# Allotting the twice-used buffers first, masking six more pairs by a bias matmul, and moving one piece of second products

## The chip, the cores and the metric

The kernel runs on one NeuronCore of a Trainium2 chip. The metric is the device time of one execution in microseconds (us), lower being better. The core has a matrix engine (TensorE, PE in the profile; its weight loads are listed apart as PEld), VectorE (DVE), ScalarE (ACT), GpSimd (POOL), SyncE (SP, which here only issues transfers) and 16 DMA engines. TensorE's results go to PSUM, eight banks of 128 x 512 float32; SBUF is the working memory of 128 partitions.

## The reference

Two blocks are computed one after the other. The first is attention with two branches over q, k and v of shape (8, 8, 576, 64): a coarse one on means of four positions, and a local one in which a position sees only those less than 4 away.

```python
q_d = q.reshape(B, H, Sd, factor, D).mean(axis=3)      # the same for k_d, v_d; factor = 4
out_up = np.repeat(sm_attn(q_d, k_d, v_d), factor, axis=2)
mask = np.abs(pos[:, None] - pos[None, :]) < factor
scores = np.where(mask, scale * np.matmul(q, k.transpose(0, 1, 3, 2)), -1000000000.0)
out = out_up + np.matmul(softmax(scores), v)
```

The second takes these outputs as x of shape (4608, 512) through two weight matrices of 512 x 2048 and 2048 x 512:

```python
h = x @ w_in
out = (h * (1.0 / (1.0 + np.exp(-h)))) @ w_out
```

## The kernel before

**Pairs.** The 64 heads are handled as 32 pairs p = 0 to 31, the two heads of a pair on the two halves of the partitions. For a pair, q and k (qkb, bf16) are transposed on TensorE (T), copied out by ScalarE (qT, kT, L583) and summed by fours on VectorE (qd, kd, L872); the scores of both branches are made by 64x64 matmuls (S, `pe_S`, L889); ScalarE takes their exponentials into Pt (local) and Pd (coarse) (L920); then come the row sums (Z), their transposes and reciprocals on VectorE (zt, r, b; L1015 to L1034), the products with v (PV), a multiply on VectorE (m, xo, L1050) and the sum of both branches on GpSimd (a, L1078), which writes the pair's part of xT. From pair 8 on these steps are bundled into visits V8 to V33 (`visit`, L1419): V(n) holds the scores of pair n, the products with v of pair n - 2, the row sums of pair n - 1 and the transposes of pair n + 1. So V31 holds the last scores, V32 the last row sums and V33 the last products with v.

**The local mask.** Scores outside the band have to vanish. For pairs below MB = 8 (L35) four matmuls come first in `pe_S`: nidn (a diagonal of -81920) against mbias (1 outside the band) puts a large negative number there, onto which the scores are added. For pairs from 8 on, Pt is multiplied by a mask of ones and zeros on VectorE after the exponential (k, L926).

**The dense part.** The 4608 rows are nine supertiles j = 0 to 8 of 512. A first product g1_j_f (L1089) is four float32 (fp32r) matmuls of 128x512, with a block of w_in as weights; its value is turned into gT by ScalarE (L1103) and VectorE (L1107). A second product g2_j_tt (L1343) is 16 bf16 matmuls in four pieces, with gT as weights and w_out as the moving operand; ScalarE copies it out (L1368) and SyncE stores it. First and second products fill TensorE between the visits.

**The last stage.** The first products of supertiles 7 and 8 are made from seven half-size products each for groups g = 0 to 7 (`prod`, P1_g to P7_g, two f32 matmuls each), with sums of blocks of w_in (S1 to S4, GpSimd, `sums`, L1169) and of xT (X1 on GpSimd, X2 to X4 on VectorE, L1166) as operands. `group` (L1233) has the copies and additions between them (p1, p5, c11, u4, c22, c12; L1236, L1237). P4_0 waits for X4 and for c22_0, which follows P7_0. `tail` (L1267) gives a fixed order of these products, in which LATE6 (L42) puts six pieces of second products of supertile 6 to fill gaps: (tt, part) = (2, 2) in group 0's step, (2, 3) and (3, 0) after it, and (3, 1), (3, 2), (3, 3) after group 1's products. `g2_part` (L1308) makes such a piece.

**Order.** A planner on the host (`Plan`) gives each step its engine, cost, due time, buffers and PSUM banks, and lists the steps of each engine; `pick` (L1523) chooses on TensorE. The program then runs each engine's list in order, with semaphores where data or buffers ask for it. So a change of one step's cost or needs can move others.

**Buffers.** SBUF is allotted in the order of the calls of `sb` (L525). Five buffers (w_in_sb, qk, vs, vq, qkb) are given back after being named, and w_in_f, qk_r, vs_r, vq_r and qkb_r get the same places under another type, for the sums of the last stage. They are the last to be allotted (L568 to L580), 142,304 bytes per partition behind w_out_bf, which is the first; w_out_bf is at a multiple of 64, and 142,304 is 32 more than one.

Of the kernel before, what the change touches and what calls it, by code (L numbers as in the profile page):

```python
# [31 lines left out]
VE, VDUE = 'ACT', 12  # L32
CAST2 = 4
SW = tuple(range(1, NPAIR))
MB = 8  # L35
LAG = 2
THR0 = 10
LEAD = 6
# [464 lines left out]
def bass_hourglass_attn__then__act_silu_kernel(  # L503
# [9 lines left out]
    with kctx:  # L513
# [11 lines left out]
        def sb(name, shape, dt, n=None):  # L525
            if n is None:
                return E(nc.sbuf_tensor(name, shape, dt))
            return [E(nc.sbuf_tensor(f"{name}{i}", shape, dt)) for i in range(n)]

        w_out_bf = sb("w_out_bf", [128, 16, 512], BF16)  # L530
        xT = sb("xT", [128, 4, XR], F32)
        gT = sb("gT", [128, 16, 512], BF16, 2)
# [31 lines left out]
        vsel = sb("vsel", [128, 3, 207], BF16)  # L564
        vend = sb("vend", [128, 2, 128], BF16)
        cv = sb("cv", [128, 16], F32)

        with contextlib.ExitStack() as early:  # L568
            E = early.enter_context
            w_in_sb = sb("w_in_sb", [128, 4, DFF], F32R)  # L570
            qk = sb("qk", [128, 2, 576], F32, N_QK)
            vs = sb("vs", [128, 10, 64], F32, N_VS)
            vq = sb("vq", [128, 4, 256], F32, N_VQ)
            qkb = sb("qkb", [128, 2, 576], BF16, N_QKB)
        E = kctx.enter_context
        w_in_f = sb("w_in_f", [128, 4, DFF], F32)
        qk_r = sb("qk_r", [128, 1152], F32R)
        vs_r = sb("vs_r", [128, 640], F32R, N_VS)
        vq_r = sb("vq_r", [128, 1024], F32R, N_VQ)
        qkb_r = sb("qkb_r", [128, 576], F32R, N_QKB)  # L580

        def copy(eng, e, out_, in_):
            return e.activation(out_, in_, AF.Copy) if eng == "ACT" else e.tensor_copy(out_, in_)  # L583
# [305 lines left out]
        def pe_S(p):  # L889
            s, bb = S("T", p), bank(("s", p))  # L890
            rl = [R(f"kT{s}"), R(f"qT{s}"), R(f"kTa{s}"), R(f"kTb{s}")]
            rd = [R(f"kd{s}"), R(f"qd{s}"), R(f"kdp{s}")]
            bias = p < MB
            if bias:
                for h in range(2):
                    for y in range(2):
                        mm(PS[half(y), bb[h], 0:288], nidn[half(h), :], mbias[half(h), y, :],
                           [R("nidn")] + [R(f"mb{i}") for i in range(4)], [rB[bb[h]]], True, False)
            for i in range(5):
                for h in range(2):  # L900
# [13 lines left out]

        def after_S(p):
            def exps(local):
                def emit(jb):
                    m, b = S("P", p), bank(("s", p))
                    d, a, e_, sc = (Pt[m], 0, 288, 0.125) if local else (Pd[m], 288, 504, 0.0078125)
                    P.op("ACT", lambda e: e.activation(d[:, :, :], PS[:, b[0]:b[1] + 1, a:e_], AF.Exp, scale=sc),  # L920
                         [rB[b[0]], rB[b[1]]], [R(f"P{m}" if local else f"Pd{m}")])
                return emit

            def emitk(jb):
                m = S("P", p)
                P.op(jb.ran, lambda e: e.tensor_tensor(  # L926
                    Pt[m][:, :, :], Pt[m][:, :, :], mask[:, :].unsqueeze(1).to_broadcast([128, 2, 288]), ALU.mult),
                    [R(f"P{m}")] + [R(f"mask{i}") for i in range(3)], [R(f"P{m}")])
            kw = dict(bank=[(("s", p), ())], take=[("P", p)], pre=[f"S{p}"], due=D(p, 6.0))
            J(f"x{p}", "ACT", 0.66, exps(True), **kw)  # L930
            J(f"xd{p}", "ACT", 0.54, exps(False), **kw)
            if p >= MB:
                J(f"k{p}", K_ENG, {"DVE": 0.46, "POOL": 1.2}, emitk, pre=[f"x{p}", "mask0", "mask1", "mask2"], use=[("P", p)], port=True,
                  due=D(p, 5.3))

# [331 lines left out]
        def tail():  # L1267
# [4 lines left out]
            for g in range(9):  # L1272
# [13 lines left out]
                    g2_lo(6)  # L1286
                if g == 1:
                    prod(g, 6, a(g), False)
                if g:
                    prod(g - 1, 4, a(g - 1), False)  # L1290
                if g < 8:
                    if not g:
                        prod(g, 2, z(g, 1), True)
                        for tt, part in LATE6[0]:
                            g2_part(LO - 1, tt, part)
                    if g != 1:
                        prod(g, 6, a(g), False)
# [10 lines left out]
        def g2_part(j, tt, part):  # L1308
            key = ("g", j, tt)

            def emit(jb):
                b = bank(key)[0]
                for f in parts(j, part):
                    mm(PS[:, b, :], gT[j % 2][:, f, 128 * tt:128 * tt + 128], w_out_bf[:, f, :],
                       [R(f"w_out{f // 4}"), R(f"g{j % 2}_{f}")], [rB[b]], f == 0, f == 15)
            chain(f"g2_{j}_{tt}_{part}", 0.866, emit, 4, [f"s{j}_{f}" for f in parts(j, part)], [(key, G2_BANKS(j))])

        def parts(j, part):
            return range(4 * part, 4 * part + 4) if j < LO else (2 * part, 2 * part + 8, 2 * part + 1, 2 * part + 9)
# [59 lines left out]
                        , bank=[(("q", p), T_BANKS(p)), (("k", p), T_BANKS(p))])  # L1379

        def sk(p):
            return dict(use=[("T", p)], pre=[f"{a}{b}{p}" for a in "em" for b in "qk"] + ["pads"] + (["nidn", "mb0", "mb1", "mb2", "mb3"] if p < MB else []), bank=[(("s", p), S_BANKS(p))])

        def zk(p):
            return dict(use=[("P", p)], pre=[f"k{p}" if p >= MB else f"x{p}", f"xd{p}"] + SELZ)

        def vk(p):
            return dict(use=[("P", p), ("vb", p), ("vd", p)], pre=[f"k{p}" if p >= MB else f"x{p}", f"xd{p}", f"cv{p}", f"vd{p}"])

        def merge(*ds):  # L1390
            o = {}
# [5 lines left out]
        def split(p):  # L1397
            J(f"T{p}", "PE", 0.42, lambda jb: pe_T(p), mm=36, kind="A", due=D(p, 8.5), **tk(p))
            after_T(p)
            if p >= SPLIT:  # L1400
                return
            J(f"S{p}", "PE", 0.46, lambda jb: pe_S(p), mm=28 + 4 * (p < MB), kind="A", due=D(p, 6.5), **sk(p))
# [16 lines left out]
        def visit(n):  # L1419
# [5 lines left out]
            if new:  # L1425
                nm = 28 * s + 36 * t + 32 * (pv is not None) + 24
            else:
                nm = 28 * s + 36 * t + 28 * (pv is not None) + 14 * (z is not None)
            if s:
# [166 lines left out]
```

## Time and profile before

| | us |
|---|---|
| median of 3 runs | 338.47 (336.92, 338.47, 339.60) |
| the profiled execution | 339.03 |
| its span in the profile | 337.1 |
| TensorE busy | 318.6 of it |
| f32 matmuls against w_in_sb, 504, busy | 128.4 |
| bf16 matmuls of second products, busy (page's group of 562) | 125.0 |
| masks on VectorE (L926), 24 | 20.8 |
| granted TensorE clock, mean | 0.985 |

The page gives for each engine the time in which an instruction of it was running. Times in the trace's timeline count from the start of the span. Matmul records overlap, since a matmul is started before the one ahead of it has drained, so the pace is read from one start to the next; a few records are missing. "Issue" is time in which an engine waited for nothing that the profile shows.

### The profile page before, as it was taken

To read this page: it belongs to the slowest core of one execution; us is meant where nothing else is said; L and a number is where in the kernel's file an instruction comes from. 1 tells how busy PE (TensorE), PEld (TensorE's weight loads), DVE (VectorE), ACT (ScalarE), POOL (GpSimd) and SP (SyncE) were. 2 spreads that over 40 slices of the span, in tenths; PEclk is the share of its full clock that TensorE was granted. 3 is DMA by queue.
4 is the path that set the end of the run, shared out by engine and by line. 5 is a ranking of instruction groups with operands and counts; after the bars stand their busy time and mean duration, and the time that the engine had idled before them with its cause. 6 is when DMAs were issued, how large, how long until landed. Compare 5 with 4: busy or idle time off the path is not lost.

```text
span 337.1 us, 11443 instructions
## 1 busy us (share of the span) xinstructions
PE 318.6 (95%) x4923; PEld 208.3 (62%) x4957; DVE 239.9 (71%) x405; ACT 189.9 (56%) x340; POOL 180.4 (54%) x237
## 2 busy tenths in 40 slices
PE   6766999999999999999999999999999999999996
PEld 2454677865555775577547755775567555676544
DVE  7758889755686976789679966997599877555400
ACT  4833856664644665476456646564566516765531
POOL 8466378417588668861687058804798482000000
PEclk9977999999999999999999999999999999999999
DMA  8999999997889967896398429600210010000042
GB/s 176 200 248 211 316 170 198 213 180 173 164 178 206 244 151 164 214 207 156 72 227 185 100 51 206 169 1 24 75 36 2 0 64 31 31 1 2 0 156 95
DMA packets 70669, 44.64 MB, mean 132 GB/s; under 512 B 45914, under 2 KB 63770, under 8 KB 70618
## 3 DMA queue, kind: packets, MB, share of 16 engines
q1 hardware_dynamic: 56714, 28.08, 32.0%
q0 software_dynamic: 13088, 15.36, 27.1%
q8 instruction: 39, 0.64, 0.8%
q10 hardware_dynamic: 816, 0.46, 0.6%
q14 instruction: 12, 0.10, 0.1%
HBM read 45.61 MB, written 9.44 MB: 163 GB/s over the span
## 4 chain that ended last, share of the span: by engine, by line
PE 89%; issue 4%; DVE 2%; ACT 2%; DMA 1%; POOL 1%; ACTq 0%; POOLq 0%
PE PS L589 85%; PE PS L837 3%; DVE xT L1166 2%; DMA qkb<-in_q_dram 1%; POOL xT L1078 1%; ACT qT L583 1%; ACT kT L583 0%; ACTq L738 0%; DVE xo L1237 0%; POOL gT L623 0%; DVE xo L1050 0%; DVE qkb L1237 0%; ACT Pt L920 0%; ACT Pd L920 0%; ACT osb L1336 0%
## 5 line engine op out<-in xcount | busy, mean ns | idle before, releaser
L589 PE MATMUL PS<-xT,w_in_sb 128*128 128x512 f32 x504 | 128.4, 403 | 0.5 <-DVE xo L1237 0.5
L589 PE MATMUL PS<-w_out_bf,gT 128*128 128x512 bf16 (+1 forms) x562 | 125.0, 373 | 3.7 <-issue 3.0
L589 PEld LDWEIGHTS PS<-xT,w_in_sb 128*128 128x128 f32 x504 | 92.3, 188 | 24.6 <-ACT osb L1368 1.0
L589 PEld LDWEIGHTS PS<-w_out_bf,gT 128*128 128x128 bf16 x592 | 54.7, 98 | 63.8 <-issue 5.2
L1103 ACT ACTIVATE th<-PS 128x512 f32<-128x512 f32 x112 | 67.0, 599 | 37.6 <-PE PS L589 23.5
L1107 DVE SCALAR_TENSOR_TENSOR gT<-th,PS 128x512 bf16<-128x512 f32 x112 | 74.1, 679 | 13.2 <-ACT th L1103 11.3
L1078 POOL TENSOR_TENSOR xT<-xo 128x576 fp32r<-128x576 f32 (+5 forms) x48 | 42.5, 900 | 27.6 <-DVE xo L1050 27.1
L583 POOL CAST vb<-vs 128x640 bf16<-128x640 f32 x32 | 23.0, 720 | 41.4 <-PE PS L589 39.2
L1368 ACT ACTIVATE osb<-PS 128x512 f32<-128x512 f32 x35 | 20.7, 597 | 42.3 <-PE PS L589 41.1
L1050 DVE TENSOR_TENSOR xo<-PS,Rb 128x720 f32<-128x720 f32 x32 | 28.8, 900 | 14.5 <-PE PS L589 14.3
L920 ACT ACTIVATE Pt<-PS 128x576 bf16<-128x576 f32 x32 | 20.9, 652 | 30.3 <-PE PS L589 30.3
L812 POOL TENSOR_TENSOR vt<-vq 128x512 f32<-128x512 f32 x24 | 31.4, 1308 | 6.8 <-DMA vq<-in_v_dram 6.6
L926 DVE TENSOR_TENSOR Pt<-Pt,mask 128x576 bf16<-128x576 bf16 x24 | 20.8, 865 | 17.9 <-ACT Pt L920 17.9
L1034 DVE STREAM_TRANSPOSE Rb<-zr 128x768 f32<-128x768 f32 x32 | 30.9, 964 | 0.2
L702 POOL DMA_DIRECT2D qkb<-in_k_dram x31 | 16.9, 547 | 17.1 <-PE PS L837 11.4
L583 ACT ACTIVATE qT<-PS 128x576 bf16<-128x576 bf16 x32 | 21.1, 660 | 8.3 <-PE PS L837 5.5
L872 DVE TENSOR_REDUCE qd<-qT 128x144 bf16<-128x576 bf16 x32 | 22.7, 711 | 2.8 <-ACT qT L583 2.8
L837 PE MATMUL PS<-idn,qkb 64*64 64x64 bf16 x1152 | 18.3, 198 | 6.2 <-issue 4.0
L872 DVE TENSOR_REDUCE kd<-kT 128x144 bf16<-128x576 bf16 x32 | 22.9, 716 | 0.0
L583 ACT ACTIVATE kT<-PS 128x576 bf16<-128x576 bf16 x32 | 21.1, 660 | 0.0
L1252 ACT ACTIVATE gT<-xo 128x512 bf16<-128x512 f32 x24 | 14.9, 627 | 10.5 <-DVE xo L1237 10.5
L702 POOL DMA_DIRECT2D qkb<-in_q_dram x31 | 17.7, 572 | 5.1 <-DMA vs<-in_v_dram 5.1
(86 smaller groups left out, 339.2 us busy)
## 6 DMA issues: line engine op xcount, KB each, us to landing
vs<-in_v_dram SPq DMA_DIRECT2D x124, 80.0 KB, 4.9
out_dram<-osb SPq DMA_DIRECT2D x35, 256.0 KB, 3.1
vq<-in_v_dram SPq DMA_DIRECT2D x24, 256.0 KB, 5.0
qkb<-in_q_dram POOLq DMA_DIRECT2D x31, 144.0 KB, 4.6
qkb<-in_k_dram POOLq DMA_DIRECT2D x30, 144.0 KB, 5.1
w_in_sb<-in_moe_w_in_dram POOLq DMA_DIRECT2D x4, 1024.0 KB, 8.4
w_out_bf<-in_moe_w_out_dram POOLq DMA_DIRECT2D x4, 512.0 KB, 12.9
vq<-in_v_dram SPq DMA_DIRECT2D x48, 32.0 KB, 4.8
```

The lines of the kernel that those rows point to most:

```text
L583: return e.activation(out_, in_, AF.Copy) if eng == "ACT" else e.tensor_copy(out_, in_)
L589: P.op("PE", lambda t: t.matmul(out_, lhsT, rhs, start=start, stop=stop, skip_group_check=True), r, w, after=fence[:])
L702: P.op(j.ran, lambda s: s.dma_start(out_(), in_()), r() if r else [], w(), sem(), after=gates(hold))
L812: P.op("POOL", lambda g: g.tensor_tensor(vt[:, :, :], vq[n][:, :, 0:128], vq[n][:, :, 128:256], ALU.add), [R(f"vqm{n}"), R(f"vqe{n}0"), R( ...
L837: P.op("PE", lambda e, o=o, w=w, j=j: e.transpose(o, w, idn[half(j), :]), [R("idn"), R(f"qkb{n}{x}")], [rB[t]])
L872: P.op("DVE", lambda e: e.tensor_reduce(dst, src.rearrange("p (g r) -> p g r", r=4), AX.X, ALU.add), [R(f"{'qk'[x]}T{s}")], [R(f"{'qk'[x]} ...
L920: P.op("ACT", lambda e: e.activation(d[:, :, :], PS[:, b[0]:b[1] + 1, a:e_], AF.Exp, scale=sc), [rB[b[0]], rB[b[1]]], [R(f"P{m}" if local ...
L1034: P.op("DVE", lambda e: e.transpose(Rb[n][:, :].rearrange("p (c q) -> p c q", q=32), zr[z][:, :].unsqueeze(2).to_broadcast([128, 24, 32])) ...
L1050: P.op("DVE", lambda e: e.tensor_tensor(xo[x][:, :, :], PS[:, bb[0]:bb[1] + 1, 0:360], Rb[u][:, :].rearrange("p (x c) -> p x c", x=2)[:, : ...
L1078: P.op("POOL", lambda g, dst=dst, in0=in0, in1=in1: g.tensor_tensor(dst, in0, in1, ALU.add), [R(f"xo{x}")], xblk(kc, t + a, t + e_))
L1103: P.op("ACT", lambda e: e.activation(th[x][:, :], PS[:, b, :], AF.Tanh, scale=0.5), [rB[b]], [R(f"th{x}")])
L1107: P.op("DVE", lambda e: e.scalar_tensor_tensor(gT[j % 2][:, f, :], th[x][:, :], 1.0, PS[:, b, :], ALU.add, ALU.mult), [rB[b], R(f"th{x}")] ...
```

## The change

Three things are changed. The five twice-used buffers and their second names are allotted ahead of everything else instead of behind it; they move to multiples of 64, and all that was ahead of them moves up by 69,632 bytes, a multiple of 64. MB becomes a set: pairs 14, 18, 22, 26, 30 and 31 are masked by the bias matmuls too, and their multiplies on VectorE go. One of the three pieces behind group 1, (3, 1), is placed ahead of P4_0, and a piece of `g2_part` now names the piece before it as needed. The costs that the planner is given follow (0.13 more for a visit with a bias).

```diff
-MB = 8
+MB = tuple(range(8)) + (14, 18, 22, 26, 30, 31)
...
+        with contextlib.ExitStack() as early:
+            E = early.enter_context
+            w_in_sb = sb("w_in_sb", [128, 4, DFF], F32R)
+            qk = sb("qk", [128, 2, 576], F32, N_QK)
+            vs = sb("vs", [128, 10, 64], F32, N_VS)
+            vq = sb("vq", [128, 4, 256], F32, N_VQ)
+            qkb = sb("qkb", [128, 2, 576], BF16, N_QKB)
+        E = kctx.enter_context
+        w_in_f = sb("w_in_f", [128, 4, DFF], F32)
+        qk_r = sb("qk_r", [128, 1152], F32R)
+        vs_r = sb("vs_r", [128, 640], F32R, N_VS)
+        vq_r = sb("vq_r", [128, 1024], F32R, N_VQ)
+        qkb_r = sb("qkb_r", [128, 576], F32R, N_QKB)
         w_out_bf = sb("w_out_bf", [128, 16, 512], BF16)
...
         cv = sb("cv", [128, 16], F32)
-
-        with contextlib.ExitStack() as early:
...
-        qkb_r = sb("qkb_r", [128, 576], F32R, N_QKB)
...
-            bias = p < MB
+            bias = p in MB
...
-            if p >= MB:
+            if p not in MB:
                 J(f"k{p}", K_ENG, {"DVE": 0.46, "POOL": 1.2}, emitk, pre=[f"x{p}", "mask0", "mask1", "mask2"], use=[("P", p)], port=True,
...
                 if g == 1:
                     prod(g, 6, a(g), False)
+                    g2_part(LO - 1, *LATE6[2][0])
                 if g:
                     prod(g - 1, 4, a(g - 1), False)
...
-                        for tt, part in LATE6[g + 1]:
+                        for tt, part in LATE6[g + 1][g:]:
                             g2_part(LO - 1, tt, part)
...
-            chain(f"g2_{j}_{tt}_{part}", 0.866, emit, 4, [f"s{j}_{f}" for f in parts(j, part)], [(key, G2_BANKS(j))])
+            chain(f"g2_{j}_{tt}_{part}", 0.866, emit, 4, [f"s{j}_{f}" for f in parts(j, part)] + ([f"g2_{j}_{tt}_{part - 1}"] if part else []), [(key, G2_BANKS(j))])
...
             if s:
-                at_ += 0.37
+                at_ += 0.37 + 0.13 * (n in MB)
```

What it does to the order of the program, beside the added matmuls and the dropped masks: up to pair 14's scores nothing moves. On TensorE, between V30 and the last stage, before: V30, nine groups of first products, V31, five groups and three pieces of supertile 6, V32, three pieces, V33, P1_0, P5_0, four pieces, P2_0, one, P6_0, two, P1_1, P5_1, P7_0, P3_0, P6_1, P4_0, P2_1, three pieces. After: V30, five groups, V31, six, V32, three groups and four pieces, V33, P1_0, P5_0, four pieces, P2_0, three, P6_0, two, P1_1, P5_1, P7_0, P3_0, P6_1, one piece, P4_0, P2_1, two pieces. On VectorE the next pair's sums of q and k (L872) move up where a mask is gone, the k sum ahead of two evictions of first products (L1107), and the steps of pairs 29 to 31 follow the visits. On ScalarE the exponentials of pair 31 come four and five copies (L1103) earlier. On SyncE one of the loads of pair 18's v slides behind the next group of vq loads. GpSimd's list is the same.

More of the change, by code (lines that the diff above doesn't have):

```diff
@@ L566, in bass_hourglass_attn__then__act_silu_kernel @@
         cv = sb("cv", [128, 16], F32)
-        with contextlib.ExitStack() as early:
[L569 to L579, printed above, removed]
-        qkb_r = sb("qkb_r", [128, 576], F32R, N_QKB)
         def copy(eng, e, out_, in_):
@@ L1381, in sk @@
         def sk(p):
-            return dict(use=[("T", p)], pre=[f"{a}{b}{p}" for a in "em" for b in "qk"] + ["pads"] + (["nidn", "mb0", "mb1", "mb2", "mb3"] if p < MB else []), bank=[(("s", p), S_BANKS(p))])
+            return dict(use=[("T", p)], pre=[f"{a}{b}{p}" for a in "em" for b in "qk"] + ["pads"] + (["nidn", "mb0", "mb1", "mb2", "mb3"] if p in MB else []), bank=[(("s", p), S_BANKS(p))])
         def zk(p):
-            return dict(use=[("P", p)], pre=[f"k{p}" if p >= MB else f"x{p}", f"xd{p}"] + SELZ)
+            return dict(use=[("P", p)], pre=[f"k{p}" if p not in MB else f"x{p}", f"xd{p}"] + SELZ)
         def vk(p):
-            return dict(use=[("P", p), ("vb", p), ("vd", p)], pre=[f"k{p}" if p >= MB else f"x{p}", f"xd{p}", f"cv{p}", f"vd{p}"])
+            return dict(use=[("P", p), ("vb", p), ("vd", p)], pre=[f"k{p}" if p not in MB else f"x{p}", f"xd{p}", f"cv{p}", f"vd{p}"])
         def merge(*ds):
@@ L1401, in split @@
                 return
-            J(f"S{p}", "PE", 0.46, lambda jb: pe_S(p), mm=28 + 4 * (p < MB), kind="A", due=D(p, 6.5), **sk(p))
+            J(f"S{p}", "PE", 0.46, lambda jb: pe_S(p), mm=28 + 4 * (p in MB), kind="A", due=D(p, 6.5), **sk(p))
             after_S(p)
@@ L1428, in visit @@
                 nm = 28 * s + 36 * t + 28 * (pv is not None) + 14 * (z is not None)
+            if s and n in MB:
+                nm += 4
             if s:
-                at_ += 0.37
+                at_ += 0.37 + 0.13 * (n in MB)
                 marks[f"S{n}"] = at_
```

## The prediction

> **What bounds the kernel now.** I read the page's busy shares first, then the busy time of each engine by stretches, then what TensorE waited for after 45 us, then its timeline where the change works. From the page, TensorE is the engine to watch:
>
> ```profile
> PE 318.6 (95%) x4923; PEld 208.3 (62%) x4957; DVE 239.9 (71%) x405; ACT 189.9 (56%) x340; POOL 180.4 (54%) x237
> PE 89%; issue 4%; DVE 2%; ACT 2%; DMA 1%; POOL 1%; ACTq 0%; POOLq 0%
> ```
>
> The second line is the chain that ended last: 89% of the span runs through TensorE, 2% through VectorE. By stretches (start:end, length, then busy of TensorE and the others, granted clock, DMA share, GB/s):
>
> ```profile
> 0.00:15.00 15.00, 9.88 (x219) 5.00 (x221) 11.09 (x46) 9.39 (x17) 9.20 (x31) 1.00 1.01 190
> 15.00:32.00 17.00, 12.63 (x380) 9.90 (x381) 12.33 (x22) 7.46 (x14) 11.08 (x15) 0.70 1.14 213
> 32.00:45.00 13.00, 11.21 (x231) 8.15 (x232) 9.67 (x17) 8.24 (x16) 7.64 (x12) 1.00 1.08 274
> 45.00:250.00 205.00, 201.42 (x3574) 132.86 (x3596) 159.53 (x254) 118.96 (x212) 130.02 (x159) 1.00 0.72 153
> ```
>
> TensorE idles 11.3 us before 45 us (5.1 + 4.4 + 1.8), where the DMA share is over 1, but only 3.6 us of the next 205. What it waited for from 45 us to the end (us in total, times, longest):
>
> ```profile
> PE PS L589 <- issue: 3.4, 20, 0.4
> PE PS L589 <- DVE xo L1237: 0.5, 1, 0.5
> ```
>
> No wait on a mask (L926), and one wait on VectorE at all. So after 45 us work added to TensorE lengthens the kernel and work removed from VectorE shortens nothing, unless the one wait or the "issue" time changes. The changed program issues the same instructions in the same order on every engine up to pair 14's scores, which stand near 102.9 us; only addresses differ before.
>
> **The masks.** Six of the 24 VectorE multiplies go: 6 x 0.865 us (20.8 us over 24) = 5.2 us of VectorE, worth nothing on the path by the list above. What moves up on VectorE behind a missing mask is the next pair's k reduction (L872), ahead of two evictions instead of behind them. If ScalarE's kT copy were late it would hold those evictions, and TensorE's next first product would want their bank; the reduction is 0.72 us and TensorE has four banks of 0.94 us in that stretch (four f32 matmuls of 0.234, below), so I take nothing, and bound it by 0.3 us at five places, 1.5 us.
>
> Added are 6 x 4 matmuls of nidn and mbias, 64x288. Rows of the same matmuls at pair 7 (start, us, what):
>
> ```profile
> 45.06 0.32 PE L589 MATMUL PS<-mbias,nidn 64*64 64x288 bf16 x4
> 45.21 0.32 PE L589 MATMUL PS<-qT,kT 64*64 64x58 bf16 x20
> ```
>
> Four of them push the scores from 45.06 to 45.21, 0.15 us; alone they show 0.32. Each group stands between a full matmul and the scores, in a stretch where TensorE has no gap, so 6 x 0.15 = +0.9 us on the path; the upper bound is 6 x 0.32 = 1.9. A gain is excluded, for no wait of TensorE names L926.
>
> **The end of attention and the moved piece.** Without a mask the last pair's visit V31 (scores) comes after 5 groups of first products instead of 9; V32 then stands 6 groups later and V33 3 groups and 4 second-product pieces after that. From V30 to V33 there were 56 f32 and 24 bf16 matmuls, now 56 and 16: V33 starts 8 x 0.217 = 1.7 us earlier (0.217 from the 20 second products between 104.28 and 108.63 us, one without a record). The moved work is put behind V33, and together with the spare piece 12 more bf16 matmuls (2.6 us) now stand between V33 and product P4_0. There the kernel of before waits (TensorE's timeline; the last bracket is idle time and its releaser):
>
> ```profile
> 275.20 0.82 PE L589 MATMUL PS<-xT,w_in_sb 128*128 128x512 f32 x2
> 275.86 1.04 PE L589 MATMUL PS<-w_out_bf,gT 128*128 128x512 bf16 x4
> 279.40 0.63 PE L589 MATMUL PS<-xT,vs_r 128*128 128x512 f32 x2
> 279.87 0.63 PE L589 MATMUL PS<-xT,vq_r 128*128 128x512 f32 x2
> 281.95 1.19 PE L589 MATMUL PS<-xT,w_in_sb 128*128 128x512 f32 x4 [0.53 <-DVE xo L1237]
> ```
>
> P4_0 waits for c22_0 on VectorE, which the chain of waits leads back through X4, u4_0, the slow X sums beside GpSimd (3.43 us for two at 274.33) and the last a31. That chain starts 1.7 us earlier, and P4_0 comes later, so -0.53 us. What is late next is c22_0 behind P7_0: between P7_0 and P4_0 stand P3_0, P6_1 and the moved piece, 0.94 + 0.87 = 1.8 us, against 0.2 of drain (0.63 less 0.47) and 0.69 of c22_0; it holds by 0.9 us. Nothing is issued by DMA in the moved steps; the one load that changes place on SP's queue (a vs piece of pair 18 behind a vq load) goes past transfers that take 4.9 us, and no TensorE wait after 45 us names a DMA.
>
> The piece puts bf16 work ahead of P4_0. The rows price that: two f32 matmuls behind bf16 ones take 275.86 - 275.20 = 0.66 us, behind f32 ones 279.87 - 279.40 = 0.47. One more such change costs +0.19. V32 now leads into f32 instead of bf16 work, bounded by another 0.1 (four f32 matmuls behind a visit at 45.56 take 1.14 to the next, against 0.94); I take 0.1. Sum after 45 us: 0.9 - 0.53 + 0.19 + 0.1 = +0.7 us.
>
> **The addresses.** w_in_sb, qk, vs, vq and qkb move from 32 bytes past a multiple of 64 to multiples of 64; all else keeps its remainder. Loads: TensorE waits 2.0 us for DMA, all before 45 us. Weight loads of TensorE (mean ns of one):
>
> ```profile
> L589 PEld LDWEIGHTS PS<-xT,w_in_sb 128*128 128x128 f32 x504 | 92.3, 188 | 24.6 <-ACT osb L1368 1.0 <-DVE xo L1237 1.0 <-DVE gT L1107 0.5
> L837 PEld LDWEIGHTS PS<-idn,qkb 64*64 64x64 bf16 x1152 | 14.6, 110 | 8.5 <-issue 4.7 <-DMA qkb<-in_k_dram 2.0 <-DMA qkb<-in_q_dram 0.9
> L589 PEld LDWEIGHTS PS<-Pd,vd 64*64 64x64 bf16 x304 | 7.6, 110 | 0.0
> ```
>
> qkb starts at the odd 32 bytes, vd does not, and both take 110 ns: no effect in bf16. For f32 no row exists, since every f32 weight buffer was at the odd 32 bytes. A load slower at the new place has no row for it either. I take 0; bounds: -9.8 us (first rival) and +1.4 (third).
>
> So the profiled execution of 339.03 us (span 337.1, 1.9 around it) would become 339.7. It stands 0.56 above the median of 338.47; the forecast is **339.1 us**, no change. Measurement of this kernel tells changes over about 1% from none (its three runs span 0.8%).
>
> **The rivals.**
>
> *Aligned f32 weights make f32 matmuls faster.* They follow each other at 0.47 / 2 = 0.234 us, bf16 ones at 0.217, though both stream 512 columns; the f32 weight load is 188 ns against 98. If alignment shortened that load by 17 ns, 560 f32 matmuls would gain up to 17.5 ns each: -9.8 us, 329.3. For it: that gap of pace. Against: the equal 110s. Half of it would already be a gain of over 1%. Chance 0.11.
>
> *TensorE starves for instructions; slower.* The instruction queue moved 39 packets of 16.4 KB for 9,880 TensorE instructions, 253 each, and the chain has "issue" pieces of 2.89 us (19.45) and 2.62 (30.84), and one of 0.39 at 173.66 among dense attention matmuls. From 127 to 147 us 1,092 instructions ran, a packet per 4.7 us. The change adds 48 and so shifts every packet boundary behind pair 14. If the boundaries fall into visits so that ten of some eleven packets come 0.4 us late, +4 us: 343. It decides once a packet takes longer than the 4.7 us per packet; against it, only one such stall of that size is seen in 205 us. Chance 0.09.
>
> *Loads into the moved buffers take longer.* The Trainium skill (DMA: Bandwidth & Descriptors, "How a descriptor splits into AXI transactions") has a piece that doesn't start at a multiple of 256 bytes cost extra beats of 32. It tells this of reads, and neither place is at such a multiple: 256 bytes at remainder 96 would be 11 beats, at 128 it is 12, an estimate from that page that speaks against the change. As a mechanism of this kernel: the loads of qkb land after 4.6 to 5.1 us, and TensorE waits for them at three places; landing 0.45 us later at each is +1.4 us, giving 340.5. Against it: DMA-bound time ends at 45 us, and the waits that name a DMA are only 2.0 us there. Chance 0.08.
>
> *The order does not do what it says.* c22_0 is still late at P4_0, because the X sums slow down beside GpSimd further: the 0.5 comes back, 339.6. Chance 0.08.
>
> **How the numbers follow.** The forecast keeps 0.64. Its own range: 337.0 (bias hidden, run-to-run low) to 341.0 (1.9 for the bias, 1.5 for banks, less half a spread). The two small rivals lie inside it. Faster by over 1% is under 335.1: 0.11 plus 0.03 for a start that happens to be shorter, since 0.70 of the clock between 15 and 32 us leaves room: 0.14. Slower, over 341.9: 0.09 plus 0.01. Within: 0.76. The range that leaves 2 in 10 out reaches a little towards the faster rival: 335.8 to 341.2.
>
> **What would show it.** Bias groups of 0.15 us ahead of pairs 14 to 31; P4_0 without a wait, its first two matmuls 0.66 us apart from the third; 18 masks; f32 pairs still 0.47 us. Weight loads of w_in_sb well under 188 ns, or f32 pairs of 0.43, prove the first rival; "issue" pieces of 0.4 us at more than three visits the second; DMA waits over 2.0 us before 45 us the third.

## The result and the profile after

| | before | changed |
|---|---|---|
| median beside each other, first chip | 338.06 (12 runs) | 335.24 (12 runs) |
| ratio, 95% interval | | 0.9914 [0.9886, 0.9943] |
| once more on another chip, ratio | | 0.9885 [0.9859, 0.9911] |
| the profiled execution, its span | 339.03, 337.1 | 334.99, 333.1 |

The ratios leave out executions more than 1.5% above the fastest of the same kernel. The change makes the kernel some 0.9 to 1.2% faster. The forecast of 339.1 us, no change, was wrong, and 335.24 lies below its range.

The page of the changed kernel, busy shares and the chain that ended last, answers to the two lines shown of before:

```profile
PE 315.9 (95%) x4947; PEld 208.5 (63%) x4981; DVE 233.4 (70%) x399; ACT 190.3 (57%) x340; POOL 179.8 (54%) x237
PE 88%; DMA 4%; issue 4%; POOL 2%; ACT 1%; ACTq 0%; POOLq 0%
```

TensorE has 24 matmul records more (4947 to 4923) and is busy 2.7 us less. Its busy total alone does not say that the work became shorter: the second profile of the changed kernel has 317.9 us, and a variant that is as fast (b_none, below) has 322.4, with more of its matmuls on record. The paces further down decide that. By stretches (start:end, length, busy of TensorE, its weight loads, VectorE, ScalarE and GpSimd, granted clock, DMA share, GB/s):

```profile
0.00:15.00 15.00, 10.31 (x261) 5.67 (x263) 9.98 (x44) 9.62 (x18) 8.72 (x30) 0.89 1.02 193
15.00:32.00 17.00, 10.81 (x380) 7.89 (x368) 13.30 (x24) 7.59 (x15) 13.41 (x19) 0.78 1.17 245
32.00:45.00 13.00, 12.89 (x245) 9.36 (x245) 10.46 (x19) 8.94 (x18) 6.52 (x10) 0.89 1.04 250
45.00:250.00 205.00, 201.80 (x3571) 135.41 (x3593) 157.24 (x253) 120.62 (x215) 131.52 (x162) 1.00 0.70 152
```

The start shows lower granted clocks in other slices than before (0.89, 0.78, 0.89 against 1.00, 0.70, 1.00); from 45 us on the clock is 1.00 in both. The clock at the start differs from one profile to the next of kernels that do the same work there, and so does the time lost: at 50 us the profiles of this study stand 2.2 us ahead of to 1.9 behind the one of before. I therefore compare single profiles from 50 us on, where the clock is full: for every matmul that two programs share, its start in the one trace less its start in the other, and how that difference moves from 50 us to the end. By that the changed kernel gains 2.75 us, in its second profile 2.59; the other 1.2 us of the first profile lie before 50 us, and I can't assign them.

What TensorE waited for from 45 us on (us in total, times, longest):

```profile
PE PS L588 <- issue: 2.5, 16, 0.2
PE PS L588 <- ACT Pt L919: 0.2, 1, 0.2
PE PS L588 <- POOL vb L582: 0.2, 1, 0.2
```

(Lines of helpers are one lower than before.) The wait for c22_0, 0.5 us, is gone, and the longest "issue" piece fell from 0.4 to 0.2. Most of these pieces are no waits. Of the 560 full-width second-product matmuls 30 have no record in the profiles of before and of the changed kernel, and each hole can show as a piece of up to 0.2 us. The profile of b_none has all 560, and its list from 45 us on has a single piece, of 0.5. The rows of before and of b_none:

```profile
L589 PE MATMUL PS<-w_out_bf,gT 128*128 128x512 bf16 x530 | 121.5, 379 | 3.7 <-issue 3.0
L588 PE MATMUL PS<-w_out_bf,gT 128*128 128x512 bf16 x560 | 127.8, 380 | 0.0
```

The bias group of pair 14 and the end of the chain that waited, in TensorE's timeline (start, us, what, count):

```profile
107.02 0.32 PE L588 MATMUL PS<-mbias,nidn 64*64 64x288 bf16 x4
107.17 0.32 PE L588 MATMUL PS<-qT,kT 64*64 64x58 bf16 x20
...
277.97 0.63 PE L588 MATMUL PS<-xT,qk_r 128*128 128x512 f32 x2
278.44 1.04 PE L588 MATMUL PS<-w_out_bf,gT 128*128 128x512 bf16 x3
279.12 1.28 PE L588 MATMUL PS<-xT,w_in_sb 128*128 128x512 f32 x4
280.25 1.90 PE L588 MATMUL PS<-w_out_bf,gT 128*128 128x512 bf16 x8
```

The group takes its 0.15 us, and the piece (one of its four records is missing) stands ahead of P4_0 (279.12), which waits for nothing. The weight loads did not get shorter (mean ns of one behind the comma):

```profile
L588 PEld LDWEIGHTS PS<-xT,w_in_sb 128*128 128x128 f32 x504 | 93.2, 189 | 21.1 <-ACT osb L1368 1.0
L836 PEld LDWEIGHTS PS<-idn,qkb 64*64 64x64 bf16 x1152 | 14.2, 110 | 6.0 <-DMA qkb<-in_k_dram 2.4 <-issue 1.4 <-DVE qkb L582 0.9
```

And yet the f32 matmuls did. The plainest place is the first long row of them, 68 without a break, in the timelines of before and of the changed kernel:

```profile
55.60 16.12 PE L589 MATMUL PS<-xT,w_in_sb 128*128 128x512 f32 x68
```

```profile
54.40 15.72 PE L588 MATMUL PS<-xT,w_in_sb 128*128 128x512 f32 x68
```

The same 68 matmuls take 0.40 us less, 6 ns each (0.40 / 67). Once the row has settled, the trace has 231 to 235 ns from one start to the next before, and 226 or 227 after. This is the gain to explain.

### The profile page after: what moved, and what is told of

It is laid out like the page before. It is cut to its first block, busy times and chain, and to the rows that moved or that the text cites. A ratio compares the mean times of both kernels' runs of the same rounds, so it can differ in the third digit from the quotient of the medians.

```text
span 333.1 us, 11486 instructions
## 1 busy us (share of the span) xinstructions
PE 315.9 (95%) x4947; PEld 208.5 (63%) x4981; DVE 233.4 (70%) x399; ACT 190.3 (57%) x340; POOL 179.8 (54%) x237
## 4 chain that ended last, share of the span: by engine, by line
PE 88%; DMA 4%; issue 4%; POOL 2%; ACT 1%; ACTq 0%; POOLq 0%
PE PS L588 85%; PE PS L836 3%; DMA vs<-in_v_dram 2%; DMA qkb<-in_q_dram 1%; DMA out_dram<-osb 1%; POOL vb L582 1%; ACT osb L1368 0%; POOL gT L622 0%; POOL w_in_sb L766 0%; ACTq L737 0%; POOL qkb L701 0%; ACT osb L1336 0%; POOL kT L631 0%; POOL kd L631 0%; POOL idw L631 0%
## 5 line engine op out<-in xcount | busy, mean ns | idle before, releaser
L588 PE MATMUL PS<-xT,w_in_sb 128*128 128x512 f32 x504 | 126.7, 400 | 0.0
L925 DVE TENSOR_TENSOR Pt<-Pt,mask 128x576 bf16<-128x576 bf16 x18 | 14.1, 784 | 18.0 <-ACT Pt L919 18.0
L836 PE MATMUL PS<-idn,qkb 64*64 64x64 bf16 x1152 | 17.5, 198 | 4.0 <-DMA qkb<-in_k_dram 2.2
```

What stands on the lines that cost most here:

```text
L588: P.op("PE", lambda t: t.matmul(out_, lhsT, rhs, start=start, stop=stop, skip_group_check=True), r, w, after=fence[:])
L836: P.op("PE", lambda e, o=o, w=w, j=j: e.transpose(o, w, idn[half(j), :]), [R("idn"), R(f"qkb{n}{x}")], [rB[t]])
```

## The experiments

All runs of the whole kernel in one table; m1 and m2, kernels of matmuls alone, follow below. "Distance" is the address of w_in_sb less that of xT, modulo 256 bytes, from the allotment (qk, vs, vq and qkb move along with w_in_sb). "Row" is the row of 68. "Pace" is the mean of the gaps between successive f32 matmuls that are under 245 ns, some 480 in a trace. "Held" is the time from 50 to 250 us in which a weight load waited for a gate product of VectorE (line 1107 before), and how often; each profile is of one execution. "From 50" is the change from 50 us on against the profile of before.

| kernel | distance | row, us | pace, ns | held, us | from 50, us | ratio of times [95%] |
|---|---|---|---|---|---|---|
| before | 224 | 16.12 | 233.1 | 0.8 (3) | | |
| changed | 0 | 15.72 | 228.2 | 1.0 (4) | -2.75 | 0.9914 [0.9886, 0.9943] |
| after_again | 0 | 15.72 | 228.3 | 1.0 (4) | -2.59 | 0.9885 [0.9859, 0.9911] |
| e1_allot | 0 | 15.72 | 228.9 | 2.9 (12) | -1.83 | 0.9942 [0.9906, 0.9978] |
| e2_no_allot | 224 | 16.13 | 233.1 | 0.6 (2) | -0.54 | 0.9997 [0.9970, 1.0025] |
| e3_pad_last | 0 | 15.71 | 228.8 | 3.8 (15) | -1.26 | 0.9940 [0.9910, 0.9970] |
| e4_shift32 | 224 | 16.13 | 233.1 | 0.4 (1) | -0.55 | 0.9972 [0.9946, 0.9999] |
| d1_both32 | 0 | 15.74 | 229.0 | 3.5 (14) | -1.62 | 0.9958 [0.9919, 0.9996] |
| d2_pad96 | 64 | 16.16 | 233.2 | 0.7 (3) | +0.20 | 1.0016 [0.9987, 1.0045] |
| b_none | 0 | 15.71 | 228.7 | 3.1 (13) | -2.17 | 0.9907 [0.9872, 0.9942] |
| b_30_31 | 0 | 15.71 | 229.1 | 2.9 (12) | -1.89 | 0.9922 [0.9887, 0.9957] |
| b_mid | 0 | 15.71 | 228.1 | 1.0 (4) | -3.54 | 0.9877 [0.9836, 0.9918] |

"From 50" is one profile each, and programs with the same instructions differ in it by up to 0.6 us (e1_allot and e3_pad_last), so a few tenths mean nothing there unless a place in the trace shows them.

### Which part of the change brings it: e1 to e4

**e1_allot** is the kernel before with the move of the allotment alone:

```diff
+        with contextlib.ExitStack() as early:
...
+        qkb_r = sb("qkb_r", [128, 576], F32R, N_QKB)
         w_out_bf = sb("w_out_bf", [128, 16, 512], BF16)
...
-        with contextlib.ExitStack() as early:
...
-        qkb_r = sb("qkb_r", [128, 576], F32R, N_QKB)
```

> The kernel before with the allotment of the twice-used buffers put first and nothing else changed: 24 masks on DVE, 8 bias pairs, the old order of the last stage. Theory A (what decides is where the f32 weights of the first product start within 64 bytes: 32 past a multiple before, on a multiple after; each of the some 500 f32 matmuls then follows the one before it some 7 ns sooner): the whole gain is here, 3 to 4 us off, some 334.5 us, ratio near 0.989, and the steady f32 pace read from start to start falls from some 233 to some 227 ns. Theory B (the gain comes from the masks that left DVE and from the moved piece): no gain, some 338 us, pace 233 ns. Theory C (the order in memory matters by something other than the remainder, for example the distance between weights and moving operand): also some 334.5 us; the third kernel of this set separates it from A.

**e2_no_allot** is the changed kernel with these two hunks taken back.

> The changed kernel with the allotment left as it was before: the six bias matmul pairs and the moved piece alone. Theory A: f32 pace stays at some 233 ns; six bias groups at 0.15 us cost 0.9, the removed wait ahead of the last piece gives back some 0.5: some 338.5 us, between 0 and 1 us above the kernel before. Theory B: some 335 us, the whole gain. Theory C: as A, some 338.5 us.

**e3_pad_last** moves the late buffers by 32 bytes in the kernel before, and nothing else:

```diff
         cv = sb("cv", [128, 16], F32)
 
+        sb("pad", [128, 8], F32)
         with contextlib.ExitStack() as early:
```

> The kernel before with 32 unused bytes per partition put ahead of the twice-used buffers, which stay last: they move by 32 bytes, from 32 past a multiple of 64 to a multiple, and no other buffer moves. Theory A: the whole gain with this alone, 3 to 4 us off, some 334.5 us, f32 pace some 227 ns. Theory B: some 338 us. Theory C: some 338 us, pace 233 ns, since order and distances are kept to within 32 bytes.

**e4_shift32** puts the early buffers of the changed kernel 32 bytes past a multiple of 64 again:

```diff
+        sb("pad", [128, 8], F32)
         with contextlib.ExitStack() as early:
...
         qkb_r = sb("qkb_r", [128, 576], F32R, N_QKB)
+        sb("pad2", [128, 8], F32)
         w_out_bf = sb("w_out_bf", [128, 16, 512], BF16)
```

> The changed kernel with 32 unused bytes ahead of the twice-used buffers, which stay first, and 32 more behind them: these buffers start 32 past a multiple of 64 again, all others keep their remainder. Theory A: the gain is lost, pace 233 ns, some 338.5 us as the second kernel. Theory B: some 335 us. Theory C: some 335 us, pace 227 ns.

Measured: the pace goes with the allotment and with nothing else. The row of 68 in e1 and e3, then in e2 and e4 (timelines):

```profile
54.41 15.72 PE L589 MATMUL PS<-xT,w_in_sb 128*128 128x512 f32 x68
```

```profile
56.74 15.71 PE L590 MATMUL PS<-xT,w_in_sb 128*128 128x512 f32 x68
```

```profile
55.17 16.13 PE L589 MATMUL PS<-xT,w_in_sb 128*128 128x512 f32 x68
```

```profile
56.96 16.13 PE L590 MATMUL PS<-xT,w_in_sb 128*128 128x512 f32 x68
```

32 unused bytes are enough to gain it (e3) or to lose it (e4), so the order of the buffers is not what counts, and theory B falls for the pace; theory C falls in the form it was put in, since e3 gains. Bias pairs and moved piece alone make no difference that the times show (0.9997). e4's times lie lower than A gave it (336.91 us where it said some 338.5), by an interval that just leaves out no change, 0.9946 to 0.9999. From 50 us on its profile and that of e2 agree to 0.01 us, so no gain of e4's own shows there, and what set its times apart stays open.

Two things in these runs spoke against a simple end. A wanted the whole gain in e1, 3 to 4 us, and it had 1.83 from 50 us on, 0.58% in the times. And e3 moves the weights on a multiple of 64 and at the same time changes their distance to xT, so it can't tell the two apart.

### What about the address counts: m1, m2, d1, d2

**m1_offsets** is a kernel of matmuls alone, the core of which is

```python
for ty, wo, mo in ORDER:          # bytes past a multiple of 64: weights, moving operand
    w, x, z = (W, X, 4) if ty == "f" else (WB, XB, 2)
    a, b = wo // z, mo // z
    for i in range(REP):                  # REP = 20
        c = a + 128 * (i % 4)
        m = t.matmul(PS[:, n % 8, :], w[:, c:c + 128], x[:, b:b + 512], start=True, stop=True, skip_group_check=True)
        n += 1
```

> A kernel of matmuls alone (none of the reference is computed, most of the output is not written): 128x128 weights against 128x512 moving values, the next weights 512 bytes on (256 for bf16), a new bank each time, 20 in a row for each setting, all settings forward and then backward. f32 weights start 0, 4, 8, 16, 24, 32, 40, 48, 56, 60, 64 and 96 bytes past a multiple of 64 with the moving operand on a multiple; the moving operand 4 to 64 bytes past it with the weights on it; three settings of both; bf16 at 0, 16 and 32. Theory A1 (only the remainder of the weights counts, and any remainder costs one step): 226.7 ns from start to start at 0 and 64, 233 ns at every other start of the weights, 226.7 at every start of the moving operand, no difference for bf16 (215 to 216). Theory A2 (the cost grows with the remainder): a slope from 226.7 at 0 to more than 233 at some. Theory A3 (the place of weights and moving operand to each other counts): both at 32 gives 226.7, and moving at 32 alone 233. Nothing shown so far says what a moving operand off a multiple does by itself: 226.7 by A1.

**m2_distance** is the same for f32 with other settings. In both, W and X start a multiple of 256 bytes apart.

> Matmuls alone again (nothing of the reference is computed, most of the output is not written), f32 only, 20 in a row for each setting, forward and backward. The first such run gave 226.7 ns with both operands on a multiple of 64 and with both 32 past one, but some 233 with the weights 64 or 96 bytes on, and 229 with the moving operand 64 on: not what a rule on the remainder of the weights alone gives. Theory R (what counts is the distance of weights and moving operand in memory, modulo some larger power of two): the weights 0 to 512 bytes on in steps of 16 give 226.7 at 0 and again at the period (512, perhaps 256 or 128) and 229 to 236 between; the moving operand alike with the opposite sign; both moved by the same 16 to 128 bytes 226.7, or close to it. Theory A (the remainder of the weights by 64): 226.7 at 64, 128, 192 and so on as at 0. Is there a distance with a pace below 226.7, a version faster than the changed kernel follows from it.

The mean of the last ten gaps of each twenty, ns, from the starts in the two traces (one execution each), forward and backward pass; a part of the settings:

```
weights at, moving at    m1              weights at, moving at    m2
  0,   0              226.7 226.7          128,   0            233.3 233.3
 16,   0              233.5 233.3          192,   0            233.4 229.2
 32,   0              233.3 233.3          240,   0            226.7 226.6
 64,   0              233.4 233.4          256,   0            226.6 226.7
 96,   0              234.6 234.6          272,   0            226.7 233.5
  0,   4              236.6 236.8          480,   0            233.5 233.2
  0,  32              233.3 233.3          512,   0            226.7 226.7
  0,  64              229.2 228.6            0, 256            226.6 226.7
 32,  32              226.7 226.7          128, 128            227.0 227.1
 16,  16              231.1 233.4          160, 128            233.3 233.4
bf16 in m1, weights at 0, 16, 32, or moving at 32: 215.8 to 215.9
```

Theory A falls: the weights at 64 and 96 are as slow as at 32. Theory R holds for the distance, with a period of 256 bytes: in m2 every start of the weights from 0 to 256, in steps of 16, has the pace of the one 256 bytes further on, to 0.1 ns in both passes. Distances of 0, 256 and 512 give 226.6 or 226.7 in both passes. Of the starts of the weights between, 240 and 496 do too; 28 and 272 do so in one pass of two and 16 in one of four (233 to 235 in the others), so what went before matters too; the rest never do.

The distance is not all. Both moved by 32, 64 or 128 bytes keep 226.6 to 227.1, but both moved by 16 are slow at a distance of 0 (230.0 and 231.0 in m2). The moving operand at 16 with the weights at 0 has 232.2 and 232.3 in m1, at a distance of 240 at which the weights alone moved are fast. R explains neither. No setting with a moving operand off a multiple of 32 bytes reached the fast pace, and no setting of all has a pace below 226.6. The bf16 pace was the same at all four settings tried. The f32 weight load is 188 ns at the fast and the slow settings alike.

Then the same in the kernel before. **d1_both32** leaves the weights 32 past a multiple of 64 and moves xT there too:

```diff
+        sb("pad", [128, 8], F32)
         xT = sb("xT", [128, 4, XR], F32)
+        sb("pad2", [128, 8], F32)
```

> The kernel before with 32 unused bytes ahead of the moving operand of the first product and 32 behind it: the twice-used buffers stay last and stay 32 past a multiple of 64, the moving operand is now also 32 past one, and the distance of the two is a multiple of 512, as in the changed kernel (in the kernel before it is 32 short of one). Nothing else changes its remainder by 64. Theory R: pace 226.7 in the long stretches, the gain of the allotment alone, as in the runs with the allotment first or the 32 bytes ahead of the late buffers: 1.3 to 1.9 us less from 50 us on, ratio near 0.994. Theory A: pace 233 ns, ratio 1.0.

**d2_pad96** is e3 with 96 bytes in place of 32 (`[128, 24]`): the weights on a multiple of 64, but at the wrong distance.

> The kernel before with 96 unused bytes ahead of the twice-used buffers: they start on a multiple of 64, as in the run with 32 bytes, but 64 past a multiple of 512 from the moving operand. Theory A: pace 226.7, ratio near 0.994. Theory R: no gain, pace 233, ratio 1.0, 0 to 0.3 us apart from 50 us on.

The row of 68 in d1, then in d2:

```profile
57.49 15.74 PE L591 MATMUL PS<-xT,w_in_sb 128*128 128x512 f32 x68
```

```profile
54.69 16.16 PE L590 MATMUL PS<-xT,w_in_sb 128*128 128x512 f32 x68
```

The distance decides in the kernel as well: d1 has the pace and 1.62 us with neither operand on a multiple of 64, d2 has neither with both on one. (d1's profiled execution is the longest of its ten, 339.19 us; its lost time lies before 50 us, and from 45 us on its clock is 1.00 like that of the others.) The remainder by 64, which the prediction and my first theory looked at, is beside the point.

### Where the rest comes from: b_none, b_30_31, b_mid, after_again

These are the changed kernel with other sets in line 35: `tuple(range(8))` alone, with (30, 31), with (14, 18, 22, 26), and unchanged.

> The changed kernel without the six added bias pairs: allotment and moved piece alone, the mask of pairs 14 to 31 on DVE as before; without them the last pair's products stand after nine groups as in the kernel before. From 50 us on, against the kernel before, the same matmuls one by one: pace 2.2 less. If the moved piece alone fills the wait ahead of the last stage's first new product (0.8 us lost there before), 0.8 less again: some 3.0, and the six bias groups cost 0.7 net in the changed kernel (2.75 from 50 us on), so this one is as fast or up to 0.3 faster: ratio near 0.991. If the wait went because the last pair's products came earlier (pairs 30 and 31 by bias), the wait is there still, 0.5 idle or more: 2.2 less, ratio near 0.9935. If the issue wait at 174 us (0.6 lost there before) went by the count of instructions, it is here still, up to 0.4 idle, since no instruction is added ahead of it.

> The changed kernel with only pairs 30 and 31 of the six added bias pairs: allotment, moved piece, and the order of the last stage as in the changed kernel. From 50 us on against the kernel before: 2.2 less by the pace, 0.8 less by the wait, 0.25 more by two bias groups: some 2.75 less, as the changed kernel, ratio near 0.991, with the four other bias groups (0.5) paid back by the issue wait at 174 us, which is here still if it goes by the count of instructions. If the masks taken off DVE in pairs 14, 18, 22 and 26 gained something by themselves, this one is slower than the changed kernel by that.

> The changed kernel once more, on the chip of the next one: ratio to the kernel before near 0.991, as the first time; from 50 us on 2.75 us less than before, give or take 0.6 for the issue wait at 174 us, which came and went between kernels with the same instructions ahead of it. Long f32 stretches: most of the starts 226 to 227 ns apart, some 1 us of weight loads held up by the gate products of DVE (line 1106) between 50 and 250 us.

> The changed kernel without the bias pairs 30 and 31: allotment, moved piece, the masks of pairs 14, 18, 22 and 26 as bias. Theory: the masks of the four pairs whose products stand next to the long f32 stretches hold up DVE's gate products there once the f32 pace is 227 ns, so these four pay; pairs 30 and 31 only cost their 0.12 each, since the moved piece alone fills the wait of the last stage. So the weight loads held up by DVE's gate products come to about 1 us from 50 to 250 us, as in the changed kernel and not 3 as in the runs without the four, and from 50 us on it is 0.2 to 0.4 us faster than the changed kernel, some 3.0 less than before: ratio near 0.990, too near to the changed kernel for the intervals to part them. Rival: pairs 30 and 31 are needed for the wait, and it is 0.5 slower than the changed kernel, with that wait back in the profile.

**The moved piece alone fills the wait.** In b_none, where the last pair is as late as before, TensorE's timeline has the piece and then P4_0 without idle time:

```profile
278.46 1.04 PE L588 MATMUL PS<-w_out_bf,gT 128*128 128x512 bf16 x4
279.15 1.27 PE L588 MATMUL PS<-xT,w_in_sb 128*128 128x512 f32 x4
```

Against e1, which lacks only the piece, that stretch is 0.8 us shorter (e1 keeps a wait of 0.53). Pairs 30 and 31 are not needed for it.

**The four masks off VectorE pay once the pace is up, in the profiles.** b_none and b_30_31 gained less than I expected (2.17 and 1.89 us against some 3.0 and 2.75). Their f32 rows are broken in places where a mask still stands on VectorE. The weight load's own list of waits from 50 to 250 us, for before, e1, the changed kernel and b_mid:

```profile
PEld PS L589 <- DVE gT L1107: 0.8, 3, 0.4
```

```profile
PEld PS L589 <- DVE gT L1107: 2.9, 12, 0.3
```

```profile
PEld PS L588 <- DVE gT L1106: 1.0, 4, 0.3
```

```profile
PEld PS L588 <- DVE gT L1106: 1.0, 4, 0.3
```

How a mask gets there, in the kernel before, at pair 14 (timeline of VectorE and of weight loads; other engines left out):

```profile
111.24 0.89 DVE L926 TENSOR_TENSOR Pt<-Pt,mask 128x576 bf16<-128x576 bf16 x1
...
112.88 1.26 DVE L1107 SCALAR_TENSOR_TENSOR gT<-th,PS 128x512 bf16<-128x512 f32 x2
...
114.06 0.97 DVE L1034 STREAM_TRANSPOSE Rb<-zr 128x768 f32<-128x768 f32 x1
114.95 1.24 DVE L1107 SCALAR_TENSOR_TENSOR gT<-th,PS 128x512 bf16<-128x512 f32 x2
115.65 1.46 PEld L589 LDWEIGHTS PS<-xT,w_in_sb 128*128 128x128 f32 x7 [0.31 <-DVE gT L1107]
```

The gate product empties the PSUM bank that the next first product needs. A mask of 0.89 us and a transpose of 0.97 put two pairs of them off, and a weight load waits 0.31 us. At 233 ns a matmul this is rare (3 times in 200 us); at 227 ns a group of four asks for its bank some 25 ns sooner (4 x 6), and VectorE falls behind 12 to 15 times. Nearly all of these holds stand in the four long rows behind pairs 14, 18, 22 and 26, two to four in each (in e1 at 114, 116 and 123 us, 152, 154 and 158, 186, 188 and 192, 221, 223 and 227). In the changed kernel, the row of which starts at 108.3 us (109.9 before), the first product comes 2.0 us behind that start in place of 3.0, and three stand ahead of the transpose in place of two:

```profile
110.27 0.67 DVE L1106 SCALAR_TENSOR_TENSOR gT<-th,PS 128x512 bf16<-128x512 f32 x1
...
111.69 1.26 DVE L1106 SCALAR_TENSOR_TENSOR gT<-th,PS 128x512 bf16<-128x512 f32 x2
...
112.87 0.97 DVE L1033 STREAM_TRANSPOSE Rb<-zr 128x768 f32<-128x768 f32 x1
```

and no load waits there; one hold is left in each of the four rows. What the masks cost can be read there. These rows have 64, 56, 56 and 56 f32 matmuls in every one of the kernels, and from first start to last they take 53.71 us together before and 53.62 in e2, which has the masks off at the old distance. At the new distance they take 53.24 in e1, 53.16 in b_none and 53.28 in b_30_31, with the masks on, and 52.27 in the changed kernel and in b_mid, 52.31 in after_again, with the masks off. So taking the four masks off is worth 0.1 us at the old pace and 0.9 to 1.0 at the new one, against some 0.5 for the four bias groups. The changed kernel differs from b_30_31 by these four pairs alone, and its profile is 0.86 us ahead from 50 us on, all of it won between 100 and 230 us. The times of the runs do not part the two (0.9914 and 0.9922), nor the changed kernel and b_none (0.9907).

Each such hold also costs the pace behind it: the gaps run through values from 224 to 240 for some six matmuls before they settle at 226 and 227 again, which fits mean paces of 228.9 in e1 and 228.2 in the changed kernel. With the four pairs (b_mid) the holds are at 1.0 us as in the changed kernel. Matched with the second profile of the changed kernel, b_mid gains 0.37 us where pairs 30 and 31 stand (expected 0.25); the other 0.6 of its lead from 50 us on lies where the two programs are the same. On one chip the two have 334.38 and 334.70 us, ratios 0.9877 and 0.9885: b_mid is not slower, and the times can't tell more.

**The issue wait at 174 us comes and goes.** Before, and in b_30_31, in which no instruction is added ahead of it (TensorE's timeline):

```profile
174.05 0.22 PE L589 MATMUL PS<-Pd,hot 64*64 64x72 bf16 x2 [0.39 <-issue]
```

```profile
172.01 0.26 PE L588 MATMUL PS<-Pd,hot 64*64 64x96 bf16 x8
172.09 0.51 PE L836 MATMUL PS<-idn,qkb 64*64 64x64 bf16 x36
```

It is gone there too, and whole in b_none (0.48). So it does not go by the count of instructions, as I had thought. Profiles of the very instructions of before differ in it as well: d2 has nothing at 174 us, but a piece of 0.73 at 145 us, where before has none. It is worth 0.6 us of the difference of the first two profiles, and I do not count it as the change's. What makes it stays open.

## Why the prediction was wrong

**The step that failed: "The addresses".** I took 0 there because 64x64 bf16 weight loads took 110 ns from buffers on and off a multiple of 64. That row is true and still there (110), and for bf16 the conclusion holds (215.8 to 215.9 at all offsets). For f32 it says nothing, and the wrong thing was looked at twice: the remainder of one buffer, where the distance of two counts, and the length of the weight load (188 before, 189 after), where the start-to-start time of the matmuls counts. Measured against e2, the same program at the other distance, the term is -2.2 us from 50 us on; in e1, with the masks still on VectorE, it is -1.8, some 0.25 of which is a shorter issue wait at 174 us. The forecast without it, +0.64 us (a ratio of 1.002), lies within e2's interval of 0.9970 to 1.0025, which would not part it from no change.

**First rival.** It had the right place and sign, and rested on the right oddity (f32 pairs at 0.234 us, bf16 at 0.217, over the same 512 columns). Its mechanism was wrong: no load got shorter. Its price, -9.8 us, was the whole gap between the paces; 4.9 ns of the 17.5 came (233.1 to 228.2), 480 times, -2.3 us. The gap that stays, 227 to 216, goes with f32 itself at every distance tried. The Trainium skill (TensorE: Matmul & The Clock Gate, "Weight-path perf modes — Fast Weight Load (FWL) and DoubleRow") has the fast weight load on for 128 weights of a type other than fp32; the rows agree, 98 ns for a bf16 load of 128 columns and 189 for f32.

**"The masks ... worth nothing on the path": wrong, and the row was in my own hands.** I argued from the list of what matmuls waited for, in which no mask and no gate product stands. The wait is booked on the weight load, and the row I quoted for it ends in "DVE gT L1107 0.5". With the old pace it was worth next to nothing (0.1 us in the four long rows of e2). With the new one the holds come wherever the masks stay (2.9 to 3.8 us in e1, e3, d1, b_none and b_30_31 against 1.0), and those five gain 1.3 to 2.2 us from 50 us on where the changed kernel and b_mid gain 2.6 to 3.5. By the four long rows 0.9 to 1.0 us of that is the masks'.

**The bias matmuls**, +0.9: in e2 the visits of pairs 14, 18, 22 and 26, from their first start to the first matmul behind, grew by 0.15, 0.12, 0.12 and 0.12; six make about 0.7. Nearly right.

**The wait at P4_0**, -0.53: gone, as said, by the piece. Its size was off: from the last start ahead of it to its own there were 0.91 us where 0.23 is usual, and 0.34 to the next, 0.8 in all; e2 regains 0.80 there. The idle time of a list leaves out what a restart costs.

**The switch from bf16 to f32**, +0.19: not there. The first start of a pair behind bf16 work is recorded early, so 0.66 against 0.47 measured where the record begins. From the last bf16 start ahead of P4_0 (279.10) to P4_0's second matmul (279.54) there are 0.44 us, one bf16 and one f32 gap.

**V32 into f32**, +0.1: the visits of 30 and 31 with it cost 0.32 in e2 against 0.25 for two bias groups. About right.

**Starvation** did not come: in the changed kernel no issue piece behind 45 us is over 0.2 us. The 3.4 us of "issue" that I counted as idle time behind 45 us were for the most part missing records: with all 560 second-product matmuls recorded, b_none shows 0.5 and b_30_31 none. **Slower loads** did not come either: qkb's q and k pieces land after 4.0 and 4.8 us, before 4.6 and 5.1. The rule of the Trainium skill that stood behind that rival (DMA: Bandwidth & Descriptors, "How a descriptor splits into AXI transactions") would have had them later, by one beat in eleven by my estimate. No lateness shows here, but e2, with the addresses of before, has 4.2 and 4.5, so two profiles would not show one of a few tenths.

**The sum from 50 us on**: pace -2.2, bias +0.7, wait -0.8, issue -0.6, together -2.9; measured -2.75. The pace term is itself a difference of two profiles, so this checks the other three only: they make -0.7, and e2 has -0.54.

## What to carry to other kernels

Where f32 matmuls follow each other with fresh weights, put weights and moving operand at a distance of a multiple of 256 bytes, the moving operand at a multiple of 32, and read the pace: 32 unused bytes in the right place were worth 0.6% here. When a matmul gets faster, look again at every engine that "has time": the four masks taken off VectorE were worth 0.1 us at the old pace and 0.9 to 1.0 at the new one. And read waits on weight loads beside those on matmuls, and paces from start to start; durations of single records told neither story. An idle piece may be a missing record: count the records first.

## What the runs showed that I had not expected

The f32 pace depends on the distance of its two operands in memory modulo 256 bytes: 226.7 ns at 0, where both lie on multiples of 32 bytes, and 228.6 to 236.8 at nearly all other places, while bf16 stays at 215.8 to 215.9 at the four settings tried. It settles only after three to some ten matmuls in a row, so rows of a dozen between other work get little: in the six rows of 14 f32 matmuls in the changed kernel's last stage six gaps of 13 are at 226 or 227, against 63 of 67 in the long row. The Trainium skill (SBUF — State Buffer, "Operand start alignment") says of its own runs on start addresses that they are about legality and timed nothing; these runs time it. What in the chip makes the period, why operands 16 bytes past a multiple of 64 are slow even at a distance of 0, and why a setting's pace can hang on the one before it stay open.
